# A DeltaNet and FFN kernel on one core: scores of the first two chunks in two parts, the first inverse's fill ahead of its load, and a new order list

## The chip, the core and the metric

The kernel runs on one core of one Trainium2 chip. Five engines run their own instruction streams and wait for each other by semaphores: TensorE (PE; its weight loads are counted apart as PEld), VectorE (DVE), ScalarE (ACT), GpSimd (POOL) and SyncE (SP), which issues every DMA of this kernel. The metric is the time of one execution on the device in microseconds; less is better. The kernel before took 546.81 us, the median of three runs (544.82 to 550.54).

## The reference

```python
def _attn_ref(q, k, v, beta):            # (4, 8, 768, 48), beta (4, 8, 768), float32
    k_n = k / (np.linalg.norm(k, axis=-1, keepdims=True) + 1e-06)
    state = np.zeros((B, H, D, D))
    for t in range(S):
        kt, vt, bt = k_n[:, :, t], v[:, :, t], beta[:, :, t, None]
        y[:, :, t] = np.einsum('bhd,bhde->bhe', q[:, :, t], state)
        v_old = np.einsum('bhde,bhd->bhe', state, kt)
        state = state + bt[:, :, :, None] * np.einsum('bhd,bhe->bhde', kt, vt - v_old)
    return y

x = attn_out.transpose(0, 2, 1, 3).reshape(3072, 384)
a = x @ w1                               # w1, w2: 384 x 1024, float64
b = x @ w2
h = a * b @ w3                           # w3: 1024 x 1024
out = h @ w_out                          # w_out: 1024 x 384
```

A recurrence over 768 tokens gives, for 4 batches and 8 heads, a state of 48 x 48 and an output for each token. Its result, 3072 x 384, goes through a feed-forward block with a product of two projections in the middle. The weights come as 64-bit floats.

## The kernel before

**Attention.** The 768 tokens are cut into 12 chunks of 64, and pairs of chunks make 6 units. In a chunk the recurrence becomes matrix products: scores of keys with keys (times beta and the norms they give a triangular matrix U) and of queries with keys (masked, the tile PT), the inverse of the triangular matrix, and a chain over the chunks that carries the state. For a chunk m the parts are called `k`, `q`, `v` (loads), `K` and `Q` (transposes of keys and queries into the tile KQ on TensorE, `by_tensor`, chunks 0 and 1), `p` and `d` (the same for later chunks, by a permuted load of eight DMAs and VectorE's transpose), `s` (`scores`: TensorE, then VectorE writes U, then PT), `u` (`to_blocks`: U into the layout of the inverse), `e` (`corner`: TensorE builds the whole inverse from its blocks), `n`, `c` (the chain) and `y` (outputs). For a unit j there are `g` and `N` (squares and norms; `N` ends with the weights wt, on which U depends) and `V` (`inverse`).

**The inverse** of a unit is done in 32 x 32 blocks, all of them side by side: a load of U into the tile Ub, a fill of a pair of PSUM banks with the unit matrix by ScalarE (two copies, L516 and L521), 31 steps of two VectorE operations each, and a way back. In units 0 and 1 the load is a VectorE transpose (L508) of columns that ScalarE (four copies for a unit) and GpSimd (two) wrote before it (L492); in units 2 to 5 it goes through DRAM: eight DMAs write Ud (L499) and one loads Ub (L510). The bank pair stays taken until the inverse is done.

**Weights.** 36 pieces `P0` to `P35` (P0 to P7 of w_out, P8 to P23 of w3, then w1 and w2) are converted from 64-bit words on the chip: a DMA into one of five raw buffers, a pair of ScalarE operations (L837, L840), a VectorE shift (L842) and a GpSimd add (L844). `t` transposes a piece of w3 on TensorE (L880) and copies it to w3T, `f` multiplies w3 with w_out (`fold`, eight products of 384 columns in two halves, L895). The first fold takes the w_out pieces in the order 0, 3, 2, 5, then 1, 4, 6, 7.

**The feed-forward block** of unit 0 is done directly (`a`, `b`, L915). Units 1 to 5 use a scheme with fewer products over sums of tokens and weights (`m`, L1117, with additions on VectorE at L1143 and L1148, on ScalarE at L1145 and on VectorE or GpSimd at L200), and `o` (L1199) multiplies with the folded weights.

**Order.** Each part is a Python generator. The string ORDER names parts, and each name advances that part to its next `yield`; so the list sets the order of instructions on each engine. A stroke behind a name (`t2'`) gives that step to the other engine (ScalarE or VectorE for copies, GpSimd or VectorE for sums), and `+3` puts three matmuls whose result nobody reads ahead of the step. `bank` hands out four PSUM banks in turn, `two_banks` pairs of others. Each DMA takes one of eight semaphores in turn, so at most eight are under way.

```python
turn = (0, 3, 2, 5, 1, 4, 6, 7) if first else (0, 3, 2, 1, 5, 4, 6, 7)
for i, kc in enumerate(turn):
    pe.matmul(
        ps[:, 0:DM], lhsT=w3Ts[jc, kc // 4][:, kc % 4 * P : kc % 4 * P + P],
        rhs=wo[:, kc], start=(i == 0), stop=(i == KF - 1),
    )
    if i == KF // 2 - 1:
        yield
```

Of the kernel before, what the change touches and what calls it, by code (L numbers as in the profile page):

```python
# [12 lines left out]
ALU = mybir.AluOpType  # L13
# [26 lines left out]
warm+3 P11 beta P2 P0 P11 P11 P11 P2 beta P3 k0 K0 P0 beta P0 P0 K0' K0 P6 P6 k1 K1 zd zd zd P2 g0 P2 P9 P3  # L40
q0 K0 K0 g0 g0 g0 g0 g0 P6 P9 g0 g0 K1 P9 P3 K1 P16 K1 q1 Q0 P10 Q0' N0 K1' P6 P16 P16 P3 Q0 Q0 Q0
P12 P13 P10 s0 N0 s0 P9 P5 s0 Q1 P10 P12 Q1' P16 zp zp P12 Q1' Q1 s0 Q1' P13 P8 p2 P5 P10 t3 s0 P13
P13 s0 s0 P1 P12 u0 u0 s1 s1 s1 s1 s1 s1 P7 P4 t2 t2' t3' u0 t5 t4 P5 t5' u1 u1 u1 V0 P8 P5 V0 P8 f1
P8 V0 t1 t1 t4 t0 t8 P17 d2 zp zp zp zp zp V0 V0 V0 V0 P14 k2 P1 P1 P1 t0 N0 t8 P4 P15 V0 P7 V0 V0
V0 P7 P17 V0 P4 V0 V0 V0 P17 P7 P4 P17 f2 f0 f2 f1 V0 s1 P14 d2 V0 V0 V0 k3 P14 P15 f2 V0 s0 g1 f0
f1 g1 P14 g1 t6 t9 P19 P18 P19 f0 t9 v0 V0 V0 g1 V0 P15 V0 P19 g1 P15 P19 zp t6 P18 P23 P22 v1 f4 f4
t7 t11 t7 V0 V0 V0 t11 g1 g1 P22 P23 f3 V0 P18 V0 V0 V0 V0 g1 P26 n0 P18 t10 V0 P23 V0 P22 V0 P20
t10 N1 n0 f3 P26 f5 f5 f3 e0 N1 e0 e0 e0 e0 p2 P20 P23 P22 d2 d2 P20 e1 e0 s2 f4 p3 P21 p3 P24 P25
e0 e0 P20 n1 t12 t15 P26 f5' s2 s2 d3 c0 c0 e1 t14 s2 e1 t14 t12 t15' P21 y0 s2 s2 d3 c0 f7 y0 P26
d3 P21 P21 d3 e1 u2 u2 u2 s1 n1 e1 c0 e1 s3 s3 s3 s3 s3 s3 y0 P27 t13 P29 c1 c1 t13' e1 P24 f6 u3 u3  # L50
u3 V1 V1 V1 V1 V1 P24 V1 V1 V1 P28 P24 e1 c1 c1 P25 P27 V1 P27 V1 P29 f7 p4 P32 y1 f7 f6 y1 P25 V1
V1 V1 V1 V1 V1 y1 P28 P25 P28 P27 b0 b0 v2 P30 P31 P28 f6 d4 V1 P29 P29 zp V1 V1 V1 P32 b3 b1 b2 b1
b3 b2 b7 d4 V1 V1 P32 V1 V1 V1 V1 b7 b4 a07 c1 a04 a07 a04 b4 a02 a00 a01 P30 a05 a02 V1 V1 V1 V1 V1
V1 V1 V1 V1 a00 n2 n2 P32 a01 P31 P30 P31 a05 a03 b5 e2 e2 e2 N1 a03 P31 P33 a06 c1 k4 p4 e2 P35 P34
k5 c2 P30 e2 d4 c2 P33 b5 d4 a00 b3 e3 g2 b3 p5 e2 a06 e2 P33 a00 g2 g2 g2 P33 b2 a03 e3 e2 P34 e3
c2 a03 c2 P35 P34 g2 P35 a02 a02 g2 b2 y2 b0 d5 e3 b0 d5 a01 g2 s4 P34 W y2 v3 P35 p5 g2 a01 N2 N2
b6 a06 b6 T T W T b6 b4 W a06 e3 n3 W s4 s4 s4 s4 d5 s4 d5 a04 e3 s4 b7 b6 b4 b7 s5 s5 s5 s5 s5 T s5
u4 v4 b5 a05 W W n3 n4 e3 s5 b5 a04 W' W S0 u5 V2 e3 c2 N2 V2 c2 V2 a07 c3 b1 a05 c3 b1 V2 V2 c3 c3
V2 a07 V2 V2 V2 V2 V2 oA0 V2 V2 y3 S0 S0' W W S0 S0 S0 n4 S0 xA0 oA0 oD0 W p6 S0 S0 S0 S0 y3 S0 S0
S0 y3 S0 xA0 oB0 oC0 V2 V2 V2 V2 V2 G1 V2 xB0 oB0 S0 G1 G1 G1 G1 c3 xA0 m10 d6 V2 V2 V2 V2 V2 xB0  # L60
xC0 oC0 xD0 m10 m10 G1 G1 G1' m10 m10 m10 m10 k6 d6 xC0 V2 V2 W xC0 V2 p6 V2 xD0 xC0 V2 W V2 m10 W
m10 m10 m10 W V2 V2 m10 m10 m10 V2 m10 m10 V2 W' m10 V2 V2 k7 W W G1 m10 m10 G1 c3 V2 e4 W m10 m10
m10 m10 m10 m10 g3 m10 m10 g3 m10 m10 m10 m10 m10 d6 g3 m10 W g3 g3 e4 g3 c4 G1 m10 m10 m10 m10 e4
c4 m10 d6 p7 m10 m10 m10 m11 e4 e4 g3 g3 G1 m10 e5 m10 m11 m11 s4 e4 c4 c4 m10 m10 m10 m10' N3 m11
# [39 lines left out]
def kernel(  # L104
# [313 lines left out]

    Ux = padded("U", [P, 2 * NR * H * C + 8], 1, 2 * NR * H * C)[0]
    Us = [Ux[:, NR * H * C * i : NR * H * C * (i + 1) + 8] for i in range(2)]  # L420

    def scores(m):
        u = Us[m % 2][:, 0 : NR * H * C].rearrange("p (r h t) -> p r h t", r=NR, h=H)
        for r in range(NR):
# [978 lines left out]
```

## Time and profile before

| | before |
|---|---|
| median of three runs | 546.81 us (544.82 to 550.54) |
| the profiled execution, and its span | 541.17 us, 539.5 us |
| mean granted clock of TensorE | 0.978 |
| TensorE busy | 513.8 us (95%) |
| VectorE, ScalarE, GpSimd busy | 403.2, 221.5, 274.7 us |
| DMA | 52.66 MB in 197593 packets, mean 98 GB/s |

The span runs from the first to the last instruction of the profiled execution. Rows of a timeline give the start, the duration, the engine, the line of the kernel, the operation with its output and inputs, their shapes, a count of instructions, and in brackets the idle time of the engine ahead of the row with what ended it. "issue" means that nothing the profile shows was waited for. A matmul in float32 leaves two records.

### The profile page before, as it was taken

What the parts mean: (1) busy time and instruction counts of PE and PEld (TensorE: products, weight loads), DVE (VectorE), ACT (ScalarE), POOL (GpSimd) and SP (SyncE); (2) the same over time, 40 slices, a digit from 0 to 9 for tenths busy, and PEclk for the clock granted to TensorE, in tenths of its full rate; (3) what the DMA queues carried; (4) which work ended last, traced back from release to release, by engine and by line L of the source; (5) the groups of instructions that cost most, each with busy time, mean ns of one, the idle gap of its engine ahead of it and who ended that gap; (6) DMA issues with size and microseconds to landing.
All of it is one profiled execution on the core that took longest, in us unless ns stands there. A gap on an engine that the chain in (4) does not pass through costs nothing.

```text
span 539.5 us, 19915 instructions
## 1 busy us (share of the span) xinstructions
PE 513.8 (95%) x8466; PEld 431.6 (80%) x8466; DVE 403.2 (75%) x880; ACT 221.5 (41%) x453; POOL 274.7 (51%) x296
## 2 busy tenths in 40 slices
PE   6679998999999999999999999999999999999997
PEld 3555567688888988889988889878899788997886
DVE  2689986898667997869987799887879845536562
ACT  3787586747523133532134333245321342312210
POOL 4575763344889996066932258361368302051150
PEclk7599998999999999999999999999999999999999
DMA  8979974767554264654444561644314320010001
GB/s 222 239 202 237 239 112 114 154 163 151 98 84 81 60 139 65 104 108 78 103 102 61 82 114 49 137 80 56 53 52 108 76 40 4 17 51 8 2 1 60
DMA packets 197593, 52.66 MB, mean 98 GB/s; under 512 B 184576, under 2 KB 191872, under 8 KB 197504
## 3 DMA queue, kind: packets, MB, share of 16 engines
q1 hardware_dynamic: 197504, 51.38, 46.1%
q8 instruction: 67, 1.10, 0.9%
q14 instruction: 22, 0.18, 0.1%
HBM read 41.25 MB, written 8.91 MB: 93 GB/s over the span
## 4 chain that ended last, share of the span: by engine, by line
PE 65%; DVE 14%; SPq 7%; DMA 6%; ACT 3%; issue 3%; POOL 1%; DVEq 0%; ACTq 0%; POOLq 0%
PE ps_f L1117 26%; PE ps_f L1199 20%; PE ps_w L687 5%; SPq L297 4%; PE ps_f L895 3%; PE ps_w L786 3%; DVE tb L530 3%; DVE ps_w L535 3%; PE ps_f L915 2%; DVE KQ L390 2%; PE ps_w L616 2%; DMA raw<-in_moe_w_dram 2%; DMA perm<-in_q_dram 1%; PE ps_w L433 1%; SPq L269 1%
## 5 line engine op out<-in xcount | busy, mean ns | idle before, releaser
L200 POOL TENSOR_TENSOR ab<-ab 128x512 f32<-128x512 f32 (+1 forms) x57 | 65.5, 1167 | 67.5 <-DVE ab L1148 33.7
L1199 PE MATMUL ps_f<-w,ab 128*128 128x192 f32 x376 | 65.1, 327 | 0.0
L1117 PE MATMUL ps_f<-xT,w1s 128*128 128x256 f32 x240 | 63.4, 388 | 0.1
L1117 PE MATMUL ps_f<-xT,w2s 128*128 128x256 f32 x240 | 61.7, 387 | 1.4 <-DVE x_room L1148 1.0
L1199 PEld LDWEIGHTS ps_f<-w,ab 128*128 128x128 f32 x376 | 61.9, 190 | 0.7
L1148 DVE TENSOR_TENSOR ab<-ab,ps_f 128x512 f32<-128x512 f32 x70 | 47.6, 682 | 17.1 <-PE ps_f L1117 15.4
L1117 PEld LDWEIGHTS ps_f<-xT,w1s 128*128 128x128 f32 x240 | 43.5, 189 | 9.6 <-ACT x_room L1145 1.8
L1117 PEld LDWEIGHTS ps_f<-xT,w2s 128*128 128x128 f32 x240 | 43.6, 189 | 9.3 <-DVE x_room L1148 1.7
L459 POOL TENSOR_TENSOR PT<-PT,smask 128x512 f32<-128x512 f32 x20 | 25.4, 1276 | 44.9 <-ACT PT L457 44.7
L1199 PE MATMUL ps_f<-room,ab 128*128 128x192 f32 x272 | 47.2, 329 | 0.0
L546 DVE TENSOR_TENSOR ps_w<-ps_w,tb 128x31 f32<-128x31 f32 (+15 forms) x124 | 43.3, 349 | 4.5
L895 PE MATMUL ps_f<-w2s,w3T 128*128 128x384 f32 x128 | 43.8, 492 | 1.5 <-POOL w2s L844 1.0
L1199 PEld LDWEIGHTS ps_f<-room,ab 128*128 128x128 f32 x272 | 44.2, 190 | 0.5
L541 DVE TENSOR_TENSOR tb<-ps_w,Ub 128x31 f32<-128x31 f32 (+15 forms) x124 | 41.8, 337 | 3.4 <-DMA Ub<-Ud 0.3
L805 ACT COPY xT<-ps_w 48x256 f32<-48x256 f32 x96 | 30.6, 366 | 33.4 <-PE ps_w L786 32.9
L200 POOL TENSOR_TENSOR xT<-xT 128x256 f32<-128x256 f32 x44 | 31.9, 740 | 20.6 <-DVE xT L200 14.7
L1117 PE MATMUL ps_f<-xT,room 128*128 128x256 f32 x160 | 39.9, 381 | 0.0
L895 PEld LDWEIGHTS ps_f<-w2s,w3T 128*128 128x128 f32 x128 | 23.4, 190 | 17.3 <-POOL w2s L844 2.4
L1148 DVE TENSOR_TENSOR x_room<-x_room,ps_f 128x512 f32<-128x512 f32 x40 | 27.2, 679 | 11.1 <-PE ps_f L1117 10.0
L1145 ACT COPY x_room<-ps_f 128x512 f32<-128x512 f32 x20 | 11.7, 586 | 55.6 <-PE ps_f L1117 45.3
L1117 PEld LDWEIGHTS ps_f<-xT,room 128*128 128x128 f32 x160 | 30.1, 190 | 4.1
L1145 ACT COPY ab<-ps_f 128x512 f32<-128x512 f32 x20 | 11.7, 586 | 49.7 <-PE ps_f L1117 49.6
(196 smaller groups left out, 1078.5 us busy)
## 6 DMA issues: line engine op xcount, KB each, us to landing
raw<-in_moe_w_dram SPq DMA_DIRECT2D x16, 512.0 KB, 5.8
ktok<-in_k_dram SPq DMA_DIRECT2D x48, 96.0 KB, 3.4
vtok<-in_v_dram SPq DMA_DIRECT2D x24, 192.0 KB, 4.2
raw<-in_moe_w_dram SPq DMA_DIRECT2D x24, 192.0 KB, 4.3
out_dram<-osb SPq DMA_DIRECT2D x46, 96.0 KB, 1.7
raw<-in_moe_w_out_dram SPq DMA_DIRECT2D x8, 384.0 KB, 4.2
perm<-in_k_dram SPq DMA_DIRECT2D x40, 64.0 KB, 3.0
perm<-in_q_dram SPq DMA_DIRECT2D x32, 64.0 KB, 2.6
```

The costliest lines, as they stand in the source:

```text
L200: (dve if other else pool).tensor_tensor(out=out, in0=x, in1=y, op=op)
L297: sync.dma_start(out=dst[quarter(2 * e + j), :, :, tb, 0:nd].rearrange("t b a d -> t (b a) d"), in_=src.rearrange("b (a e) t d -> e (b a) ...
L459: pool.tensor_tensor(out=PT, in0=PT, in1=smask[:].unsqueeze(1).to_broadcast([P, H, C]), op=ALU.mult)
L541: dve.tensor_tensor(out=tv, in0=V[:, 0 : s + 1, s : s + 1].to_broadcast([P, s + 1, n]), in1=U[:, s, s + 1 : BS].unsqueeze(1).to_broadcast( ...
L546: dve.tensor_tensor(out=o, in0=o, in1=tv, op=ALU.subtract)
L687: pe.matmul(out(ps, r, h, z), lhsT=lhs(r, h, z), rhs=rhs(r, h, z), start=True, stop=True,)
L805: act.copy(out=xT[f, cc, p:NP:2, b : b + NR, :].rearrange("p a r t -> p r a t"), in_=pyv[f, z, b : b + NR],)
L895: pe.matmul(ps[:, 0:DM], lhsT=w3Ts[jc, kc // 4][:, kc % 4 * P : kc % 4 * P + P], rhs=wo[:, kc], start=(i == 0), stop=(i == KF - 1),)
L1117: pe.matmul(ps[:, n * g : n * g + n].rearrange("p (b c t) -> p b c t", b=HB, c=2), lhsT=product_weights(i, 2 * r + g), rhs=of[i], start=na ...
L1145: act.copy(out=t, in_=cell(what[1]))
L1148: dve.tensor_tensor(out=t, in0=t, in1=cell(what[2]), op=op)
L1199: pe.matmul(ps[b][:, b, :], lhsT=block(u, HF * f + i, z)[:, P * b : P * b + P], rhs=ws_[w][:, i], start=first and i == 0 and (b == 0 or n ...
```

## The change

It has three parts. First, the scores of chunks 0 and 1 are made by a new function, `early_scores`. The key products of both token groups of a chunk go into one bank pair, with two VectorE operations behind them that write U (part `s0`, `s1`, five yields fewer than before). The query products, ScalarE's copy to PT and GpSimd's mask are parts of their own, `h0` and `h1`. In the even heads a 128-column product (keys and queries beside each other) becomes two of 64 columns. Second, the inverse of unit 0 fills its banks ahead of its load. Third, ORDER is written anew from its first to its last line.

```diff
 ORDER = """
-warm+3 P11 beta P2 P0 P11 P11 P11 P2 beta P3 k0 K0 P0 beta P0 P0 K0' K0 P6 P6 k1 K1 zd zd zd P2 g0 P2 P9 P3
-q0 K0 K0 g0 g0 g0 g0 g0 P6 P9 g0 g0 K1 P9 P3 K1 P16 K1 q1 Q0 P10 Q0' N0 K1' P6 P16 P16 P3 Q0 Q0 Q0
...
+zd zd zp zp P10 P10 P10 P10 beta beta beta P0 P0 P0 P0 k0
+K0 k1 K0 P16 zd P16 g0 g0 g0 g0 P16 P16 K1 K1' K1 K0'
...
+    def by_weight(m, r, x):
+        u = Us[m % 2][:, 0 : NR * H * C].rearrange("p (r h t) -> p r h t", r=NR, h=H)
+        dve.tensor_tensor(
+            out=by_parity(u[:, r]), in0=x,
+            in1=by_parity(scale_of(ws, m)[:, r].unsqueeze(2)).to_broadcast([P, NP, 2, C]),
+            op=ALU.mult,
+        )
+
+    def early_scores(m, j):
+        KQ = KQs[m]
+        ps = two_banks()
+        fill(ps[:, 0])
+        for r in range(NR):
+            for h in range(H):
+                for z in range(2):
+                    x = KQ[feat(h % 2), NR * z + r, h // 2]
+                    n = 128 * (h // 2) + C * r
+                    pe.matmul(
+                        ps[half(z ^ (j if h % 2 else 0)), h % 2, n : n + C],
+                        lhsT=x[:, 0, :], rhs=x[:, j, :], start=True, stop=True,
+                    )
+        yield
+        psv = ps[:].rearrange("p e (a r t) -> p a e r t", a=NP, r=NR)
+        if j == 0:
+            for r in range(NR):
+                by_weight(m, r, psv[:, :, :, r, :])
+                yield
+            return
+        PTs[m] = in_turn(work, [P, NR, H, C], "PT", 3, "PT")
+        for r in range(NR):
+            act.copy(out=by_parity(PTs[m][:, r]), in_=psv[:, :, :, r, :])
+            yield
+            by_mask(PTs[m][:, r])
+            yield
...
     def inverse(j):
+        def load():
+            if j in TURNED:
+                dve.transpose(out=U[:], in_=columns().rearrange("p t m g -> p t (m g)"))
+            else:
+                sync.dma_start(out=U[:], in_=Uds.pop(j)[:])
+
         U = in_turn(work, [P, BS, BS], "Ub", 1, "Ub")
-        if j in TURNED:
-            dve.transpose(out=U[:], in_=columns().rearrange("p t m g -> p t (m g)"))
-        else:
-            sync.dma_start(out=U[:], in_=Uds.pop(j)[:])
-        yield
+        if j:
+            load()
+            yield
...
+        if j == 0:
+            load()
+            yield
...
-        parts[f"s{m}"] = lambda m=m: scores(m)
+        parts[f"s{m}"] = lambda m=m: scores(m) if m > 1 else early_scores(m, 0)
...
+        parts[f"h{m}"] = lambda m=m: early_scores(m, 1)
```

Lines of the new kernel lie 47 to 85 behind those of the old: L445 (U) becomes L476, L492 becomes L570, L508 becomes L586, L516 and L521 become L598 and L603, L530 and L535 become L615 and L620, L837 to L844 become L922 to L929, L880 becomes L965, L895 becomes L980. The rows that follow give an instruction's line, operation, output and inputs, the size, and a count.

On VectorE, from the first U to the first inverse step, stood before (U_103 is the tile U, w and w2s are weight pieces):

```order
L445 TENSOR_TENSOR U_103<-ps_w,wt 128x512
L842 TENSOR_SCALAR w_330<-w_330 128x512
L204 COPY KQ<-ps_f 48x8x64
L842 TENSOR_SCALAR w_420<-w_420 128x512
L204 COPY KQ<-ps_f 48x8x64 x2
L842 TENSOR_SCALAR w_432<-w_432 128x512
L445 TENSOR_TENSOR U_103<-ps_w,wt 128x512 x3
L204 COPY w3T<-ps_f 128x512 x2
L842 TENSOR_SCALAR w2s<-w2s 128x384
L204 COPY w3T<-ps_f 128x512
L508 STREAM_TRANSPOSE Ub<-xT_79 128x1024
```

and stands now, from the norm weights on:

```order
L417 TENSOR_TENSOR wt<-wt,ps_f 128x32
L927 TENSOR_SCALAR w_322<-w_322 128x512
L927 TENSOR_SCALAR w2s<-w2s 128x384
L476 TENSOR_TENSOR U_103<-ps_w,wt 128x512
L251 COPY KQ<-ps_f 48x8x64
L476 TENSOR_TENSOR U_103<-ps_w,wt 128x512 x3
L927 TENSOR_SCALAR w_407<-w_407 128x512
L927 TENSOR_SCALAR w2s<-w2s 128x384
L927 TENSOR_SCALAR w_403<-w_403 128x512
L251 COPY KQ<-ps_f 48x8x64
L927 TENSOR_SCALAR w2s<-w2s 128x384
L251 COPY KQ<-ps_f 48x8x64
```

One KQ copy and no weight shift is left between the first U and the other three, where three of each stood. Behind the last U come shifts and copies, then the transpose (L586).

On ScalarE, around the columns of unit 0 and the fill of the first inverse, stood before (PT is the query scores, eye the unit matrix):

```order
L457 COPY PT<-ps_w 128x512
L492 COPY xT_79<-U_103 96x32x16
L457 COPY PT<-ps_w 128x512
L492 COPY xT_79<-U_103 32x32x16
L492 COPY xT_79<-U_103 96x32x16
L492 COPY xT_79<-U_103 32x32x16
L837 ACTIVATE w_574<-raw 128x512
L840 ACTIVATE raw<-raw 128x512
L516 COPY ps_w<-eye 128x1023
L521 COPY ps_w<-eye 128x1
L204 COPY w3T<-ps_f 128x512 x2
```

and stands now:

```order
L570 COPY xT_79<-U_103 32x32x16
L922 ACTIVATE w_562<-raw 128x512
L925 ACTIVATE raw<-raw 128x512
L251 COPY w3T<-ps_f 128x512
L504 COPY PT<-ps_w 128x512 x2
L598 COPY ps_w<-eye 128x1023
L603 COPY ps_w<-eye 128x1
L363 COPY wt<-wt 128x16
L365 COPY wt<-wt 64x16 x2
L922 ACTIVATE w2s<-raw 128x384
L925 ACTIVATE raw<-raw 128x384
L251 COPY w3T<-ps_f 128x512 x2
```

The PT copies come behind the last column copy, and the fill behind them; the pair on `w2s` behind the three norm copies is piece P5 of w_out.

On SP, around the permuted loads of chunk 2, stood before (P5 is the single w_out row, ahead of them):

```order
L829 DMA raw<-in_moe_w_out_dram 128x768
L829 DMA raw<-in_moe_w_dram 128x1024
L297 DMA perm_95<-in_k_dram 32x16x32 x2
L297 DMA perm_95<-in_k_dram 32x16x16 x2
L297 DMA perm_95<-in_k_dram 32x16x32 x2
L297 DMA perm_95<-in_k_dram 32x16x16 x2
L829 DMA raw<-in_moe_w_out_dram 128x768 x3
```

and stands now:

```order
L914 DMA raw<-in_moe_w_out_dram 128x768
L914 DMA raw<-in_moe_w_dram 128x1024
L344 DMA perm_95<-in_k_dram 32x16x32 x2
L344 DMA perm_95<-in_k_dram 32x16x16 x2
L344 DMA perm_95<-in_k_dram 32x16x32 x2
L344 DMA perm_95<-in_k_dram 32x16x16 x2
L914 DMA raw<-in_moe_w_out_dram 128x768
L914 DMA raw<-in_moe_w_dram 128x1024
L914 DMA raw<-in_moe_w_out_dram 128x768 x3
```

The w_out row directly behind the permuted loads is P5 now, and a w3 piece, P8, and three more w_out pieces, with P1 the first of them, follow it. The w_out row ahead of the loads is another piece.

180 lines of the change are left out of this document (111 added, 69 removed).

## The prediction

> **What bounds the kernel now.** I read the page's busy times first, then the stretches, then the engines' rows where TensorE is idle.
>
> ```profile
> span 539.5 us, 19915 instructions
> PE 513.8 (95%) x8466; PEld 431.6 (80%) x8466; DVE 403.2 (75%) x880; ACT 221.5 (41%) x453; POOL 274.7 (51%) x296
> ```
>
> TensorE works for 513.8 of 539.5 us. A new order can win only the other 25.7 us, and time lost to a low clock. The table by stretches (start:end, length, then busy time of PE, PEld, DVE, ACT and POOL, the granted clock, the DMA share and GB/s) tells where these are:
>
> ```profile
> 0.00:13.50 13.50, 8.14 (x84) 4.79 (x84) 3.64 (x8) 5.05 (x8) 6.36 (x17) 0.80 0.88 222
> 13.50:27.00 13.50, 8.14 (x202) 6.88 (x206) 8.81 (x26) 9.60 (x20) 6.95 (x9) 0.50 0.98 240
> 27.00:40.50 13.50, 10.46 (x216) 7.92 (x209) 11.29 (x20) 11.37 (x17) 9.74 (x8) 0.94 0.73 200
> 67.50:81.00 13.50, 12.70 (x270) 8.58 (x268) 10.82 (x33) 10.75 (x18) 8.94 (x9) 1.00 0.72 111
> 81.00:94.40 13.40, 12.03 (x381) 9.88 (x382) 8.34 (x14) 9.37 (x18) 5.21 (x6) 0.87 0.48 114
> 94.40:108.00 13.60, 12.56 (x327) 8.61 (x319) 11.67 (x31) 10.50 (x20) 4.91 (x4) 1.00 0.76 153
> 108.00:515.00 407.00, 404.03 (x6798) 350.27 (x6797) 312.30 (x667) 145.19 (x315) 208.91 (x218) 1.00 0.40 77
> ```
>
> The first three rows hold 5.4 + 5.4 + 3.0 = 13.8 us of idle TensorE, 67.5 to 108 holds 0.8 + 1.4 + 1.0 = 3.2, the 407 us of the body only 3.0; the rest lies mostly at the very end. The change aims at the start. There two lines of work run toward the first corner product e0 at 74.97, and TensorE's rows (start, duration, count, and in brackets the idle time and its releaser; a matmul leaves two records) show one of them:
>
> ```profile
> 39.99 0.91 PE L895 MATMUL ps_f<-w2s,w3T 128*128 128x384 f32 x2 [0.75 <-POOL w2s L844]
> 41.90 1.26 PE L880 MATMUL ps_f<-ident,w 128*128 128x128 f32 x8 [0.56 <-POOL w L844]
> 43.00 5.97 PE L895 MATMUL ps_f<-w2s,w3T 128*128 128x384 f32 x18
> 74.97 0.73 PE L616 MATMUL ps_w<-T,U 33*33 33x32 f32 x62
> ```
>
> These are the folds w3·w_out. From 43.00 on TensorE has 44 of their products (0.66 us each: 5.97 us over 9) and five transposes (0.6: 1.26 over two) before e0: 29.0 + 3.0 of the 32.0 us. So e0 comes at 75 if the second half of the first fold starts at 43 and nothing else holds it. The other line is VectorE's: scores times weights (L445, the tile U), U turned into columns (L492), the transpose (L508), 31 inverse steps (L530, L535), the transpose back (L549), then T for e0.
>
> ```profile
> 27.47 0.19 DVE L370 TENSOR_TENSOR wt<-wt,ps_f 128x32 f32<-128x32 f32 x1
> 28.37 0.42 DVE L842 TENSOR_SCALAR w<-w 128x512 uint32<-128x512 uint32 x1
> 35.10 0.69 DVE L445 TENSOR_TENSOR U<-ps_w,wt 128x512 f32<-128x512 f32 x1 [1.26 <-PE ps_w L439]
> 38.87 1.25 DVE L508 STREAM_TRANSPOSE Ub<-xT 128x1024 f32<-128x1024 f32 x1 [0.36 <-POOL xT L492]
> 41.11 0.19 DVE L530 TENSOR_TENSOR tb<-ps_w,Ub 128x31 f32<-128x31 f32 x1
> 73.97 0.70 DVE L599 STREAM_TRANSPOSE T<-TT 128x512 f32<-128x512 f32 x1
> ```
>
> T is done at 74.67, 0.3 us before TensorE reaches e0. **Both lines end together**: to bring e0 forward the change must shorten both.
>
> **The inverse's line.** Its start hangs on loads. 13.73 MB in the first 60 us are 229 GB/s:
>
> ```profile
> DMA packets 22506, 13.73 MB, mean 229 GB/s; under 512 B 19707, under 2 KB 19707, under 8 KB 22499
> raw<-in_moe_w_dram SPq DMA_DIRECT2D x14, 512.0 KB, 5.9
> raw<-in_moe_w_out_dram SPq DMA_DIRECT2D x8, 384.0 KB, 4.2
> ktok<-in_k_dram SPq DMA_DIRECT2D x16, 96.0 KB, 5.0
> 14.76 1.94 PE L404 MATMUL ps_f<-ident,ktok 64*48 64x64 f32 x58 [0.58 <-DMA ktok<-in_k_dram]
> 20.21 1.95 PE L404 MATMUL ps_f<-ident,X 64*48 64x64 f32 x62 [1.46 <-DMA X<-in_q_dram]
> ```
>
> Adding the bytes queued up to the end of k1 (one w3 piece, beta, four w_out pieces, eight k loads: 2.9 MB, 12.7 us) and 2.5 us for the start and the last landing gives 15.2 where the row shows 14.8, so the estimate is good to a microsecond. Afterwards one w3 and one w_out piece stand ahead instead (1.8 MB): k1 at 10.4, q0 at 14.4 instead of 20.2. The norm weights, 27.66 before, follow k1 by a few operations and come at about 21.5. Now all four U are due at once, since their key products no longer stand behind Q1 and the second chunk's halves: four of 0.69 us and four other VectorE operations in between give 25.5 for the last, 10 us earlier than 35.79.
>
> Little of that arrives. ScalarE and GpSimd do the column copies behind other rows:
>
> ```profile
> 33.73 1.12 ACT L492 COPY xT<-U 96x512 f32<-96x512 f32 x1
> 34.74 0.60 ACT L457 COPY PT<-ps_w 128x512 f32<-128x512 f32 x1
> 35.37 3.34 ACT L492 COPY xT<-U 32x512 f32<-32x512 f32 x3
> 38.73 0.67 ACT L837 ACTIVATE w<-raw 128x512 f32<-128x512 f32 x1
> 39.31 0.66 ACT L840 ACTIVATE raw<-raw 128x512 uint32<-128x512 uint32 x1
> 39.87 1.01 ACT L516 COPY ps_w<-eye 128x1023 f32<-128x1023 f32 x1
> 37.75 1.08 POOL L492 COPY xT<-U 32x512 f32<-32x512 f32 x1
> 38.92 1.02 POOL L844 TENSOR_TENSOR w2s<-w2s,raw 128x384 uint32<-128x384 uint32 x1
> ```
>
> ScalarE's four copies (4 x 1.11) stand among piece conversions (a pair is 1.3, for the narrower w_out pieces 1.0) and two KQ copies (0.6 like the PT copy) and end at some 32.5. GpSimd's two stand behind five adds (1.0 for 384 columns, so some 1.35 for 512) and six memsets, and the second ends at about 34.2. The transpose then ends at 35.4. The fill, 1.0 and a short second copy (0.2, as the 32-column row of VectorE), comes behind the columns, a conversion pair (1.3), a w3T copy and two PT copies (0.6 each), and ends at 36.8. It is ahead of the transpose only in the list. So the first inverse step comes at 36.8, not 41.11: **4.3 us earlier**. The bounds are 0 (the copies stay behind GpSimd's adds) and 12 (two copies and the transpose follow U at once: 25.5 + 2.2 + 1.3).
>
> **The folds' line.** Here P5, the w_out piece of the first fold's fourth product, moves on SP from ahead of the eight perm DMAs to behind them:
>
> ```profile
> 22.32 0.38 SPq L829 DMA_DIRECT2D raw<-in_moe_w_out_dram  x1
> 25.89 7.54 SPq L297 DMA_DIRECT2D perm<-in_k_dram  x8
> ```
>
> These take 7.54 us from about 25, so P5 is issued at about 32.5 and lands at 36.7 (4.2 above). Its ScalarE pair (1.0) now stands behind the fill and three small norm copies (0.2 each) and ends at 38.5. VectorE's shift and GpSimd's add (0.4 and 1.0) give 39.9, and that fourth product was at 39.99 before. P1, for the second half, follows with its pair behind two w3T copies and P8's pair (38.5 + 1.1 + 1.3 + 1.0 = 41.9), then 0.4 and 1.0: 43.3, against 43.00. Then the same 44 products and five transposes come: e0 at **75.3, +0.3**. The bounds are -2 (P1 meets no queue) and +3 (P5 and P1 each meet one 1.3 us operation more). T, 4.3 us earlier at about 70.4, then waits for TensorE.
>
> **Score matmuls.** 32 products of 128 columns become 64 of 64. They lie before the folds, where TensorE idles 13.8 us, and cost 0 there; uncovered, 32 more at the 0.06 us apart of the 64-column row at 20.21 (1.95 over 31) would be 2 us, kept as bound. Warm-up matmuls (three, 4.29 us at the half clock at 1.65) go from the start to the gap before the first fold, where TensorE would wait for P13.
>
> ```profile
> 1.65 4.29 PE L194 MATMUL ps_f<-ident 128*128 128x512 f32 x6 [1.65 <-POOL ident masks.py:199]
> ```
>
> The clock was 0.50 from 13.5 to 27 us, though, and 0.94 in the next stretch, where matmuls stood thicker. If the score products end by 27 and only transposes follow, the folds may start at 0.5. [...]
>
> **After e0.** The largest waits of 67.5 to 108 are these:
>
> ```profile
> 81.80 0.31 PE L687 MATMUL ps_w<-vtok,TT 64*64 64x48 f32 x2 [1.51 <-issue]
> 95.25 0.73 PE L687 MATMUL ps_w<-S,KQ 48*64 48x48 f32 x35 [0.67 <-issue]
> ```
>
> They are "issue" waits inside or between products with no releaser: an earlier chain does not free them, a new order may. The clock of 0.87 costs 0.13 x 13.4 = 1.7 more. Bounds -4 (all of these) and +2 (one more such drop); I take -0.6, the size of the shorter one.
>
> **The body and the end.** The body's list is new throughout, with 3.0 us of idle to win. Units 2 to 5 load their inverse through DRAM, and VectorE's first step waits there:
>
> ```profile
> 385.21 0.68 DVE L445 TENSOR_TENSOR U<-ps_w,wt 128x512 f32<-128x512 f32 x1
> 394.63 0.19 DVE L541 TENSOR_TENSOR tb<-ps_w,Ub 128x31 f32<-128x31 f32 x1 [0.15 <-DMA Ub<-Ud]
> ```
>
> The way from U to the first step is 8.7 us in unit 5. The new list puts the first steps directly behind load and fill. Summed from the durations of such rows, VectorE has about 6.5 us of work between in unit 2, 9.5 in unit 3, 10 in unit 4 and 7 in unit 5, so it stands waiting about 2 us each in units 2 and 5, with the evacuations of TensorE's banks queued behind. Four rotating banks cover most: +0.5, bounds -2 (most of the idle time) and +4 (both waits reach TensorE). The last two units' products keep their order on TensorE: 0 (bounds -0.5 and +0.5).
>
> Sum: +0.3 + 0 - 0.6 + 0.5 + 0 = +0.2 on the profiled execution's 541.17 gives 541.4. The median of the three runs was 546.81, 5.6 above; with the same distance the time is **547.0**. A change of 1% (5.5 us) is about what a measurement of this kernel can tell.
>
> **Rivals.** *Faster: both lines move.* If P1 is ready by 41 and the clock is full by the first fold, e0 comes 2 earlier; with the waits and the low clock of 81 to 94 gone (-3.2) and 1.5 won in the body, the time is 547 - 6.7 = 540. For it: 13.8 us of idle lie there to be used. Against: P5 stands behind the perm loads.
> *Slower: the weight conversions arrive late.* One mechanism at one place: P5 and P1 are at the end of the queues of SP, ScalarE and GpSimd. Each microsecond after 43.3 goes one to one into e0, as TensorE has no slack from there to 75. If the perm DMAs start 3 us later because the raw buffer ahead of them is not free, and the clock costs the folds what it costs the stretch from 81 (1.7), e0 comes at 80, and with 2 of waits in the body: +7, 554. It decides from P1's add ending at 48.
> *It does not do what it says*: U comes early, but the column copies keep their place behind conversions and the inverse starts at 41. Folds and inverse end together as before: 547 to 549.
>
> **How the numbers follow.** The first case (hidden behind the folds) has 0.42, with its own range 543.5 to 550.5. No earlier inverse has 0.10, the faster rival 0.23, the slower 0.25. Within 1% are the first and the third, with some of the rivals' near ends: 0.54; faster 0.22, slower 0.24. The range of 539.5 to 553.5 reaches to the faster rival's time and to just short of the slower's, with about a tenth left out on each side.
>
> **What would show it.** Last U near 25.5 (hidden or not), first inverse step near 37, fourth fold product near 40, second half of the first fold near 43.3, e0 near 75.3, T ready some 4 us before. If e0 stands at 72 or 79, the fold's line is mis-sized. If e0 is right and the time is off by over 3 us, the body's list is: then the idle time of TensorE between 108 and 515, now 3.0, shows it by releaser.

## The result and the profile after

The changed kernel takes 553.61 us (median of 16 runs, 550.54 to 560.5), the kernel before 546.46 in the same series. The ratio is **1.0147, with a 95% interval of 1.0122 to 1.0173**: slower by some 8 us. (This ratio and those below leave out executions that lie over 1.5% above the fastest of the same kernel, so they are not quite the quotient of the medians.) The forecast was 547.0 with a range up to 553.5.

The profiled execution took 554.23 us, its span 552.5. From the page of the changed kernel (busy time of PE, PEld, DVE, ACT, POOL; the instruction queue q8: packets, MB, share):

```profile
span 552.5 us, 20019 instructions
PE 515.7 (93%) x8530; PEld 432.7 (78%) x8530; DVE 406.6 (74%) x883; ACT 221.9 (40%) x454; POOL 269.4 (49%) x292
q8 instruction: 67, 1.10, 0.9%
```

The start went nearly as worked out up to the first inverse step and the folds. VectorE's and TensorE's rows of the changed kernel:

```profile
24.75 1.89 DVE L476 TENSOR_TENSOR U<-ps_w,wt 128x512 f32<-128x512 f32 x3
35.45 1.23 DVE L586 STREAM_TRANSPOSE Ub<-xT 128x1024 f32<-128x1024 f32 x1
37.01 0.19 DVE L615 TENSOR_TENSOR tb<-ps_w,Ub 128x31 f32<-128x31 f32 x1 [0.33 <-ACT ps_w L603]
39.89 0.63 PE L965 MATMUL ps_f<-ident,w 128*128 128x128 f32 x4 [1.26 <-ACT w3T L251]
40.35 2.78 PE L980 MATMUL ps_f<-w2s,w3T 128*128 128x384 f32 x8
43.41 13.07 PE L980 MATMUL ps_f<-w2s,w3T 128*128 128x384 f32 x40
75.41 0.76 PE L701 MATMUL ps_w<-T,U 33*33 33x32 f32 x64
```

The last U ends at 26.6, the first inverse step is at 37.01, 4.1 us earlier than before, the next run of fold products at 43.41, and e0 at 75.41 where it was at 74.97. So 0.4 us of the loss lies ahead of e0, and all the rest behind it. The stretches of the changed kernel behind e0 (length, then busy time of PE, PEld, DVE, ACT, POOL, clock, DMA share, GB/s):

```profile
76.00:108.00 32.00, 26.33 (x765) 19.49 (x752) 20.84 (x41) 23.93 (x40) 18.21 (x17) 0.89 0.67 139
108.00:515.00 407.00, 399.01 (x6872) 343.50 (x6871) 310.75 (x670) 144.75 (x316) 198.91 (x211) 1.00 0.42 78
```

and the first of them in the kernel before:

```profile
76.00:108.00 32.00, 28.79 (x877) 22.13 (x878) 22.89 (x49) 23.61 (x44) 14.60 (x14) 0.95 0.66 139
```

TensorE stands idle 2.5 us longer from 76 to 108, and 5.0 us longer in the body (3.0 before, 8.0 now). Its long waits there have one thing in common, the word in the brackets:

```profile
83.13 0.27 PE L965 MATMUL ps_f<-ident,w 128*128 128x128 f32 x1 [3.22 <-issue]
96.96 0.21 PE L525 MATMUL ps_w<-KQ 48*64 48x64 f32 x1 [1.06 <-issue]
159.40 0.33 PE L525 MATMUL ps_w<-KQ 48*64 48x64 f32 x3 [1.46 <-issue]
242.16 0.27 PE L525 MATMUL ps_w<-KQ 48*64 48x64 f32 x2 [1.64 <-issue]
373.42 0.44 PE L772 MATMUL ps_w<-S,KQ 48*64 48x48 f32 x13 [0.79 <-issue]
```

The profile shows no semaphore that held these matmuls. All issue waits of over 0.15 us behind e0 sum to 8.6 us, against 2.5 in the kernel before; waits for another engine sum to 4.0 against 2.8. The clock's own rows have 10.2 us at half speed behind e0 (from 85, 98 and 160 on), against 3.4, which by estimate is another (10.2 - 3.4) / 2 = 3.4 us: in the kernel before, pairs of 128-column score records start 0.21 us apart at 25.18 to 26.03, at half speed, and 0.11 apart at 29.12 to 29.34, at full. Together with e0: 6.1 + 1.2 + 3.4 + 0.4 = 11.1 of the 13.0 us between the two spans; the other 1.9 us I can't assign. The two profiled executions stand further apart than the medians.

**The theory, F.** The instruction queue moved 67 packets of 16 KB. TensorE's 8530 matmul records and as many weight loads make 17060 instructions, 255 a packet; that these are what the packets hold is read from this count, and the expectations take it as 256. A float32 matmul leaves two matmul records and two weight loads, four instructions, so a block, as such a packet is called here, holds some 64 matmuls. By the packets' times in the trace, each long issue wait ends 2.2 to 3 us after such a packet starts: at 80.60, 94.05, 157.15, 239.85 and 370.96 for the five rows above. So by this theory TensorE waited for its own instructions. The changed kernel has 32 more score matmuls, half a block, and a new list, so the blocks begin at other instructions. **The rival, O**: the waits belong to the order of the work, and would come wherever blocks begin.

### The profile page after: what moved, and what is told of

The parts are those of the page before. It is cut to its first block, busy times and chain, and to the rows that moved or that the text cites. A ratio compares the mean times of both kernels' runs of the same rounds, so it can differ in the third digit from the quotient of the medians.

```text
span 552.5 us, 20019 instructions
## 1 busy us (share of the span) xinstructions
PE 515.7 (93%) x8530; PEld 432.7 (78%) x8530; DVE 406.6 (74%) x883; ACT 221.9 (40%) x454; POOL 269.4 (49%) x292
## 4 chain that ended last, share of the span: by engine, by line
PE 67%; DVE 12%; SPq 7%; DMA 6%; issue 5%; POOL 2%; ACT 1%; DVEq 0%; POOLq 0%; ACTq 0%
PE ps_f L1202 29%; PE ps_f L1284 15%; PE ps_w L772 6%; PE ps_f L1000 5%; SPq L344 4%; PE ps_w L871 3%; PE ps_w L701 2%; PE ps_f L980 2%; PE ps_w L519 2%; DMA raw<-in_moe_w_dram 2%; DVE tb L626 1%; DVE ps_w L620 1%; DVE tb L615 1%; PE ps_w L525 1%; DVE ps_w L631 1%
## 5 line engine op out<-in xcount | busy, mean ns | idle before, releaser
L1202 PEld LDWEIGHTS ps_f<-xT,w1s 128*128 128x128 f32 x240 | 43.1, 189 | 11.1 <-ACT x_room L1230 1.8
L631 DVE TENSOR_TENSOR ps_w<-ps_w,tb 128x31 f32<-128x31 f32 (+15 forms) x124 | 43.3, 349 | 4.5
L980 PE MATMUL ps_f<-w2s,w3T 128*128 128x384 f32 x128 | 44.7, 502 | 0.3 <-issue 0.3
L980 PEld LDWEIGHTS ps_f<-w2s,w3T 128*128 128x128 f32 x128 | 24.2, 196 | 16.1 <-issue 2.1
L437 DVE STREAM_TRANSPOSE KQ<-perm 128x512 f32<-128x512 f32 x36 | 24.4, 696 | 12.0 <-PE ps_w L871 4.7
```

The costliest lines, as they stand in the source:

```text
L437: dve.transpose(out=KQ[:, bs, :, i, :].rearrange("p b a t -> p (b a) t"), in_=src[:, bs].rearrange("p b a x d -> p (b a) (x d)"),)
L631: dve.tensor_tensor(out=o, in0=o, in1=tv, op=ALU.subtract)
L980: pe.matmul(ps[:, 0:DM], lhsT=w3Ts[jc, kc // 4][:, kc % 4 * P : kc % 4 * P + P], rhs=wo[:, kc], start=(i == 0), stop=(i == KF - 1),)
L1202: pe.matmul(ps[:, n * g : n * g + n].rearrange("p (b c t) -> p b c t", b=HB, c=2), lhsT=product_weights(i, 2 * r + g), rhs=of[i], start=na ...
```

## The experiments

### Half a block at the start of the kernel before

```diff
-warm+3 P11 beta P2
+warm+3 pad P11 beta P2
...
+    def pad():
+        ps = bank([P, CW])[:]
+        for _ in range(32):
+            pe.matmul(ps[0:BS, 0:BS], lhsT=ident[0:BS, 0:BS], rhs=ident[0:BS, 0:BS],
+                      start=True, stop=True)
+        for _ in range(3):
+            skip("f")
+        yield
```

> The kernel before with 32 small unread matmuls (32x32) at its idle start, behind the warm-up: 128 instructions of TensorE more (four to a float32 matmul), half of one 16 KB instruction block, and nothing else. Theory F (the issue waits are late instruction blocks: 67 packets of 16 KB in the instruction queue are 17152 instructions, and the long issue waits of both traces end 2.2 to 3 us after such a packet starts): the blocks now begin elsewhere in the same order, so the issue waits after 75 us, 2.5 us in the profile before (1.51, 0.32, 0.67), come at other places and with another sum, anything from 0 to 8 us, and the time moves by as much. Theory O (the waits belong to the order of the list): the same issue waits at the same places, 2.5 us, time 546.5 within 1 us (the 32 matmuls take some 2 us of TensorE's idle time).

Measured: 550.85 us, ratio **1.0154 (1.0093 to 1.0216)**. The matmuls themselves took 2.2 us, in idle time, and e0 came at 75.16, 0.2 later than before. Behind it, in the same order of work, stand these waits:

```profile
81.04 0.33 PE L927 MATMUL ps_f<-ident,w 128*128 128x128 f32 x1 [2.13 <-issue]
98.66 0.26 PE L663 MATMUL ps_w<-TT,late 64*33 64x32 f32 x1 [2.10 <-issue]
373.36 0.68 PE L734 MATMUL ps_w<-vtok,TT 64*64 64x48 f32 x31 [1.53 <-issue]
```

The issue waits sum to 6.8 us, at other instructions than before, and 6.8 us ran at half clock. Theory F's forecast came, theory O's did not: filler that is as good as free at its own place costs as much as the whole change. Whether any filler at the start costs, wherever the blocks lie, is asked further down.

### The two halves of the two lists

The list of the one kernel up to e0's first product, and the other's remaining steps in their order behind it: above, the changed list goes on with the old one, below it the old list with the changed one. The second of the three has 32 unread matmuls ahead of Q0 in addition, so that with the 32 more of the scores it is one block off, not half a block.

```diff
 e0 e0 e0 e0 P20 e0
-P22 P22 P22 p3 d2 P20 d2 e0
+P22 P22 P26 P23 P22 n0 P26 f3
...
 e0 N1 e0 e0 e0 e0
-p2 P20 P23 P22 d2 d2 P20 e1
+zp f4 P20 p2 f5 n1 P20 p3
```

> The changed kernel up to the first corner product e0 of its list, and from there the list of the kernel before (with the query scores of chunk 1 at their old place). The start of the changed list cost 0.4 us up to e0, so theory O (the loss lies in the new list behind e0) gives 546 to 547.5 and idle times as before: 3.2 us between 67.5 and 108, 3 us in the body. Theory F: the 32 more score matmuls put the instruction blocks half a block off against the kernel before, so the issue waits behind e0 are not those of before; the time may lie anywhere from 544 to 553. Had the start after all been what costs (a colder clock, a fuller DMA queue behind e0), it would be 553.

> The same with 32 small unread matmuls at TensorE's idle time ahead of the first query transposes: 64 matmuls more than before in all, one whole instruction block, so behind e0 the blocks begin at the same instructions as in the kernel before. Theory F: the issue waits behind e0 are those of before again (about 1.5 at the first state products and 0.7, 2.5 us in all), time 546 to 548. Theory O: the same as without the 32.

> The kernel before up to e0 and from there the changed list. Theory O: the loss is all in the part behind e0, so 552 to 554, with the waits of the changed kernel (3.2 us idle near 80, 1.5 near 158, 1.6 near 241). Theory F: the blocks begin half a block off against the changed kernel, so the issue waits differ in place and size; between 544 and 553, and what is left of the loss with issue waits set aside (0.5 to 0.6 us waits for GpSimd and VectorE) is under 2.5 us.

Measured: 1.0198 (1.0132 to 1.0264) for the new start with the old rest, 1.014 (1.007 to 1.021) with the filler, 1.0191 (1.0137 to 1.0246) for the old start with the new rest. Theory O is out in its plain form: the new start with the old rest should have been as fast as before, and lost 2%. But 554.0 us for the new start is close to the 553 expected if the start costs by what it leaves behind e0, and 552.3 us for the new rest is what theory O expected. Theory F missed its own mark with the new rest: the span, 548.6, lies 9.1 us above the one before; the issue waits make 4.1 - 2.5 = 1.6 of it and waits for other engines 7.4 - 2.8 = 4.6, so far more than 2.5 us is left with the issue waits set aside.

Theory F is not cleanly shown by the run with the filler either. The filler stood in the wrong place: it took 3.59 us at 17.77, and the key products behind it stopped for 3.34 us more, until 2.9 us after an instruction packet had started at 25.54:

```profile
28.41 1.55 PE L491 MATMUL ps_w<-KQ 48*64 48x64 f32 x47 [3.34 <-issue]
```

So the last three U began at 30.02, not 25.68, though the norm weights were there no later (23.14 and 23.56), and e0 came at 79.96 where it was at 75.79 without. From e0 to the end it takes 471.1 us (551.1 - 79.96) against 477.6 without, 477.1 in the changed kernel and 464.5 before. It has issue waits of 0.9 us only, less than the 2.5 expected, but 8.3 us of waits for other engines and 10.2 us at half clock. Without the 5.1 us that the half clock costs, 466.0 us are left, as with the old start at such a place (466.7 and 468.3 us in two runs further down, with next to no half clock). So nothing there says that the new start costs behind e0 by itself, but for a colder clock, which this run can't exclude.

### A whole block at the start, with nothing else changed

The three wide warm-up matmuls (12 instructions) give way to 67 small ones (268), which take 7.35 us at 1.65 where the three took 4.29; the list is otherwise that of the kernel before.

```diff
-warm+3 P11 beta P2
+pad P11 beta P2
...
-        for _ in range(32):
+        for _ in range(67):
```

> The kernel before with its three warm-up matmuls replaced by 67 small unread ones (32x32): 12 instructions go, 268 come, 256 more in all, exactly one instruction block, in about the same 5 us of TensorE's idle start. Behind them every block begins at the same instruction as in the kernel before. Theory F: the issue waits are those of the kernel before again (about 1.5 at the first state products near 80 and 0.7 near 95, 2.5 us behind 60 us), one or two stretches of half clock behind 60 us, and the time is 544 to 548 where half a block gave +7.5. Theory P (any filler at the start costs, by the clock, the loads or the order of arrival, not by the blocks): again +5 to +8, 551 to 554.

Measured: 544.7 us beside 545.0, ratio **1.000 (0.9956 to 1.0043)**. Half a block costs 1.5%, a whole one nothing. The start was put off by as much in both: the first matmuls on beta began at 9.11 with half a block and at 9.06 with a whole one, 6.01 before, so it isn't filler as such that costs. The largest issue wait stands at the same instruction as before, ahead of the last two records of the state products; this is the row of the kernel with the whole block, beside the one at 81.80 in the prediction:

```profile
81.67 0.31 PE L734 MATMUL ps_w<-vtok,TT 64*64 64x48 f32 x2 [0.84 <-issue]
```

Its sum of issue waits was smaller than expected, 0.8 us, and it had more waits for other engines (7.6 us) in the profiled execution, so that the spans differ by 4 us while the times of the runs do not.

### Quarters of a block, in both kernels

In the kernel before the warm-up gives way to 19 or 51 small matmuls (64 or 192 instructions more); in the changed kernel 16, 32 or 48 stand ahead of everything, while TensorE waits for beta.

```diff
-warm+3 P11 beta P2
+pad P11 beta P2
```

```diff
-zd zd zp zp P10
+pad zd zd zp zp P10
```

> The kernel before with its three warm-up matmuls replaced by 19 small unread ones: 64 instructions more behind them, a quarter of a block; the list is unchanged. Theory F (instruction blocks): waits of its own, anything from 544 to 558; with the other three places (546 for none, 550.9 for a half, and the next run) it tells whether the old list is better than the new one at all places or only at its own. Theory that only the old list's own place is good: 549 to 555.

> The same with 51, three quarters of a block. The new list had ratios of 1.0147, 1.032, 1.017 and 1.015 at its four places (mean 1.020). If the old list's mean over its four places is 1.005 or less, the new list loses about 1.5% by itself (its dense products stand closer together, whatever the place); if it is 1.012 or more, at least half of the loss is the old list's lucky place.

> The changed kernel with 16 small unread matmuls ahead of everything, while TensorE waits for beta: 64 instructions, a quarter of a block. Theory F: the issue waits (8.5 us behind 60 us in the changed kernel: 3.22, 0.32, 1.06, 1.46, 1.64, 0.79) change in place and sum, each still ending 2.2 to 3 us after an instruction packet starts; the time moves by as much, 547 to 558. Theory O (the new list itself costs): 553.6 within 1.5 us, the same waits.

> The same with 32 (half a block). Theory F: other waits again, between 546 and 558; theory O: 553.6 within 1.5 us.

> The same with 48 (three quarters of a block). Theory F: other waits again, between 546 and 558; theory O: 553.6 within 1.5 us. If over the four places of the blocks the changed kernel's mean stays above 550, its list is worse than the old one on the whole; if one of the four comes to 547 or less, the place of the blocks alone makes the loss.

| blocks moved by | old list, ratio | new list, ratio |
|---|---|---|
| 0 | 1 | 1.0147 (1.0122 to 1.0173) |
| a quarter | 1.0073 (1.0026 to 1.0119) | 1.0317 (1.0245 to 1.039) |
| a half | 1.0154 (1.0093 to 1.0216) | 1.0172 (1.011 to 1.0233) |
| three quarters | 1.0112 (1.0061 to 1.0163) | 1.015 (1.0116 to 1.0184) |
| a whole | 1.000 (0.9956 to 1.0043) | not run |
| mean of the first four | 1.0085 | 1.0197 |

The old list was at its best place, and no other of these four reaches it. The new list loses at each of its four, and no place brings it to 547 or less. Neither of the two marks set for the old list's mean, 1.005 and 1.012, is reached: it lies between. The loss of 1.47% can be put as 1.12 (difference of the means) + 0.85 (the old list's own place against its mean) - 0.50 (the new list's own place against its mean). Part of the 1.0317 is not the blocks' doing, since e0 came at 77.86 there, 2.4 us late; without it the new list's mean would be some 0.1% less. Theory F's range for a quarter block in the new list, 547 to 558 us, was missed: it took 563.27. Issue waits alone don't make the new list worse in the mean: behind e0 they are 8.6, 11.8, 5.7 and 5.2 us at its four places, but 2.5, 6.8 and 7.5 at none, a half and three quarters of the old one (one execution each). No run took the new list apart at a fixed place; a pair of traces below shows one more part of the difference.

### The two parts of code without the new list

The changed code with the old list: the first three steps of s0 and s1 stand where these stood, and h0 and h1 where their other five did. The warm-up gives way to 35 small matmuls, and with the 32 more of the scores that is a whole block.

```diff
-warm+3 P11 beta P2
+pad P11 beta P2
...
 Q1' Q1
-s0
+h0
 Q1' P13
...
-P13 s0 s0 P1 P12 u0 u0 s1 s1 s1 s1 s1 s1
+P13 h0 h0 P1 P12 u0 u0 s1 s1 s1 h1 h1 h1
```

> The two changes of code alone, scores in two parts and the fill ahead of the load, with the old list (the first three steps of s0 and s1 stand where those stood, the other five as h0 and h1 where the rest stood), and the warm-up replaced by 35 small matmuls, so that with the 32 more score matmuls one whole block is added. By theory F the blocks behind e0 begin where they did: 545 to 548, e0 at 75 to 76 (the folds bind, the code parts are hidden). If the two parts of code cost by themselves: 549 or more with e0 at 77 or later.

Measured: 545.56 beside 545.11, ratio **1.000 (0.9967 to 1.0033)**. The scores in two parts and the early fill neither win nor lose by themselves. Here are its e0 and its largest issue wait, at the same state products as in the kernel before:

```profile
77.10 0.73 PE L701 MATMUL ps_w<-T,U 33*33 33x32 f32 x62
84.55 0.31 PE L772 MATMUL ps_w<-vtok,TT 64*64 64x48 f32 x3 [2.13 <-issue]
```

e0 came at 77.1, 2.1 us later than before and later than expected, and the time was the same all the same.

### The changed kernel once more

> The changed kernel once more, for a second profile. Theory F: the same issue waits at the same instructions (L965 near 80, L525 near 96, 158 and 241, L772 near 373), each within some tenths of 3.2, 1.1, 1.5, 1.6 and 0.8 us. If they are chance, they lie elsewhere.

Measured: 552.43 us, 1.0117 (1.0058 to 1.0175). The second profiled execution has a span of 546.5 us instead of 552.5. Its waits stand at the same instructions, down to the count of records behind them:

```profile
79.82 0.27 PE L965 MATMUL ps_f<-ident,w 128*128 128x128 f32 x1 [0.96 <-issue]
93.32 0.21 PE L525 MATMUL ps_w<-KQ 48*64 48x64 f32 x1 [0.79 <-issue]
155.17 0.33 PE L525 MATMUL ps_w<-KQ 48*64 48x64 f32 x3 [0.92 <-issue]
235.25 0.27 PE L525 MATMUL ps_w<-KQ 48*64 48x64 f32 x2 [0.26 <-issue]
366.53 0.44 PE L772 MATMUL ps_w<-S,KQ 48*64 48x48 f32 x13 [0.49 <-issue]
```

So in these two executions their places are fixed by the program. Their sizes are not (3.22 became 0.96, 1.64 became 0.26, and there is one more of 1.19 at 84), against what was expected. Nothing behind e0 ran at half clock this time. Waits of 5.3 instead of 8.6 us and 5.1 us less of lost clock (10.2 / 2) are more than the difference of the two spans: this is how far executions of one kernel lie apart.

This trace can be held against the one of the section before: the same code in the old list (but for the warm-up), as many matmul records behind e0, both at full clock. From e0 to the end, first the old list, then the new:

```profile
77.10:543.80 466.70, 452.38 (x7857) 390.68 (x7856) 345.59 (x734) 170.63 (x361) 230.28 (x237) 1.00 0.40 79
74.36:546.50 472.14, 455.36 (x7856) 390.53 (x7856) 350.58 (x739) 173.12 (x364) 226.26 (x233) 1.00 0.40 78
```

The new list takes 5.4 us longer. 3.0 us of it is not waiting but busy time of TensorE, for the same products in another order, and 2.4 us is idle time, with issue waits of 5.3 against 2.3 us. (The ends of matmuls are modelled in a profile, so 3.0 is an estimate.) What in the order makes it is not shown.

### What makes a block late

First, 64 small matmuls, a whole block, at two places of the old list: ahead of the first product of s8, and ahead of a product of m30 that begins a bank.

```diff
-c6 c6 s8 m21 m21
+c6 c6 s8+64 m21 m21
...
-m30
+m30+64
```

> The kernel before with 64 small unread matmuls (one whole block each) at two places of the body: ahead of the first scores of chunk 8, near 290 us, between the chain's and the scores' small products, and ahead of a wide feed-forward product of unit 3, near 330 us, between products of 256 columns. By their rows at the start each takes 2.2 us by itself. Theory D (the blocks come too late only where many small products follow each other, since a block of 256 instructions is used up faster than the next one comes): an issue wait of over 0.8 us with or right behind the 64 at 290, none over 0.3 at 330. Theory Q (a block is late because data transfers are ahead of it, whatever is computed): waits by what SP moves there, not by the place.

Measured: 557.35 us, 1.0213 (1.0116 to 1.031), and the time a block of these takes was expected wrongly. The 64 took 4.2 to 4.8 us, not 2.2 (the row of the start was for 32). The second of the places came at 359.4, not near 330. There was a wait of 0.24 us at the first place and none at the second:

```profile
292.04 2.24 PE L242 MATMUL ps_w<-ident 32*32 32x32 f32 x65
294.51 2.34 PE L242 MATMUL ps_w<-ident 32*32 32x32 f32 x63 [0.24 <-issue]
```

Theory D (blocks are late only among many small products) is not supported by it, but it wasn't tested either: the shortest time between two instruction packets in all traces is 3.3 us, and a block that takes 4.2 us to use up can come in time.

Then 192, three blocks, at two places among wide products, in m30 and in m51, and faster: they alternate between partitions 0 to 31 and 64 to 95, and took 17 ns a record (152 in 2.59 us, in the rows below) where those of the run before took 34 (65 in 2.24 us):

```diff
-m30
+m30+192
...
-m51
+m51+192
...
+                x = slice(C * (i % 2), C * (i % 2) + BS)
+                pe.matmul(
+                    ps[x, 0:BS], lhsT=ident[x, x], rhs=ident[x, x],
+                    start=True, stop=True, skip_group_check=True,
+                )
```

> The kernel before with 192 unread 32x32 matmuls (three whole blocks) at each of two places among the wide products of 256 columns: in unit 3, near 357 us, and in the last unit, near 500 us, where hardly any data is moved (DMA share 0.02). They alternate between the two halves of the array, as the corner's products do, which took 0.73 us for 64 records. In the run before this the 64 at one place were no fair test: they ran one behind the other, 4.2 us to a block, and the shortest time between two instruction packets in all traces is 3.3 us. Theory R (TensorE waits wherever it uses up blocks faster than one in 3.3 to 4 us, data transfers or not): at some 11 to 17 ns a record the three blocks are used up in 4 to 7 us, and issue waits of 2 to 6 us in sum come at both places. Theory Q (a block is late only when data transfers are ahead of it): no wait over 0.3 near 500.

Measured: 568.28 us, 1.0435 (1.0241 to 1.0628). In the timeline of TensorE, at the two places:

```profile
348.22 2.59 PE L243 MATMUL ps_f<-ident 32*32 32x32 f32 x152
352.15 2.48 PE L243 MATMUL ps_f<-ident 32*32 32x32 f32 x128 [1.33 <-issue]
356.15 2.98 PE L243 MATMUL ps_f<-ident 32*32 32x32 f32 x104 [1.52 <-issue]
...
521.24 4.67 PE L243 MATMUL ps_f<-ident 32*32 32x32 f32 x270
527.71 3.11 PE L243 MATMUL ps_f<-ident 32*32 32x32 f32 x114 [1.81 <-issue]
```

and the two stretches, of which the first moves next to no data (DMA share 0.02, behind the clock):

```profile
520.00:531.00 11.00, 9.19 (x391) 8.35 (x390) 1.37 (x2) 0.12 (x1) 1.26 (x1) 0.86 0.02 4
349.00:360.00 11.00, 8.14 (x350) 7.75 (x343) 0.14 (x1) 0.00 (x0) 1.27 (x1) 0.72 0.40 93
```

The waits came at both places, 2.9 us in sum at the one and 1.8 at the other, the last a little under what was expected. **Theory R's forecast came: TensorE waited where it used up its instructions faster than blocks come (128 records with their weight loads, a block, in 2.48 us at 352.15, where packets start 3.3 us apart at the least), with data transfers beside it or without.** That transfers lengthen such a wait is not excluded, as the place with a DMA share of 0.40 has the longer ones.

Nor is fast use the only way to such a wait. The longest one of the changed kernel, 3.22 us at 83.13, came after a stretch of wide fold products:

```profile
53.70:80.60 26.90, 24.68 (x260) 15.71 (x259) 24.18 (x67) 15.31 (x29) 17.56 (x19) 1.00 0.84 172
```

One packet had started at 53.68, the next started only at 80.60, 0.7 us after TensorE had stopped, with twice the instructions of a block used in between (260 matmul records and 259 weight loads). The packet was late there though nothing was used up fast. The DMA engines' share was 1.03 from 75 to 80.6; that data transfers held the packet up (theory Q) fits, and is not tested. In 22 of the 82 waits counted below, the packet before lies over 8 us back.

## Why the prediction was wrong

**Right: the time of e0.** Last U 26.6 (25.5 forecast), first inverse step 37.01 (36.8), fold products from 43.41 (43.3), e0 75.41 (75.3). The rival "it does not do what it says" fell in its cause, an inverse that starts at 41, though its outcome, that folds and inverse end together, came (see below). The first fold was late: its fourth product began at 42.3 where 40 was said, as the fold itself began only at 40.35, behind a wait of 1.26 us for a w3T copy; what follows did not move with it.

**Luck: the working behind 43.3.** The prediction takes the products there for the second half of the first fold, which needs P1. But the list goes `f1`, `t0`, `f2`: at 43.41 stands the first half of the second fold, with pieces 0, 3, 2, 1 in turn, and P1 is first used at 45.34. Its add ended at 44.60, 1.3 us later than said, and cost nothing. The row at 43.41 follows directly on the transposes of `t0` at 42.97. The prediction's row of the kernel before, at 43.00, is the second fold too.

**Wrong: "T, 4.3 us earlier", hidden behind the folds.** These are VectorE's transposes back (the kernel before, then the changed one) and the changed kernel's T, which was at 73.97:

```profile
69.36 1.24 DVE L549 STREAM_TRANSPOSE Ub<-ps_w 128x1024 f32<-128x1024 f32 x1
69.45 1.24 DVE L634 STREAM_TRANSPOSE Ub<-ps_w 128x1024 f32<-128x1024 f32 x1
74.65 0.70 DVE L684 STREAM_TRANSPOSE T<-TT 128x512 f32<-128x512 f32 x1
```

The inverse began 4.1 us earlier and ended when it had ended before. From its first step to the transpose back VectorE took 32.4 us instead of 28.3: the new list gives it more work in between (29.7 us busy, 26.7 before), and it waits 0.9 us for a piece of ScalarE at 38.87. T was done at 75.35, not 70.4, and 0.06 us ahead of e0. Both lines end together again, so the 4 us were not hidden but spent; e0 came right because the folds' line did.

**Wrong, and the step that failed: what lies behind e0.** The sum has "after e0" at -0.6 and the body at +0.5, together -0.1 us. From e0 to the end the changed kernel took 477.1 us, and 472.1 in the second execution, against 464.5. The row of 1.51 <-issue was seen and read as something that "a new order may" free; no bound let such waits grow, since the +2 there stands for the clock. It was the first sign of a price: issue waits behind e0 grew from 2.5 to 8.6 us (5.3 in the second execution), and the clock cost 3.4 us more (nothing in the second). From 76 to 108 the idle time grew by 2.5 us, and the clock fell from 0.95 to 0.89, 1.9 us more by 0.06 x 32. The time without a releaser should have been a mechanism of its own in the sum, with a price on both sides, not a remainder. The prediction's last sign, e0 right and the time off by over 3 us, pointed to this place.

**Wrong: the term for the score matmuls, as a rule.** The step said that they "cost 0 there", since TensorE idles where they stand, and bounded them by the time they take. Their own time is free indeed (1.000 with a whole block). But by theory F the 128 instructions move the begin of every block behind them, and 32 matmuls with no use and no wait cost 1.5% in the old list. What this shift cost in the new list is not shown: with half a block more, which makes the shift a whole one, it took 1.0172, no less than 1.0147. The measured loss is 1.1% between the means of the two lists, 0.85% for the old list's good place, and 0.5% back; the first of the three stays open but for the 3.0 us of busy time.

**Wrong in size: the body, +0.5 with a bound of +4.** TensorE's idle time from 108 to 515 grew by 5.0 us, 3.9 of it in the three issue waits at 159, 242 and 373, and 3.4 us at half clock from 160 on cost 1.7. VectorE's waits for Ub were there as said, but smaller: 1.8 us in all, the longest 1.2, where two of about 2 were expected.

**The slower case had a chance of 0.24, for a reason that did not happen: P1's add ended at 44.60, not at 48.** Half of its second reason, the clock, was right: half clock did cost, in 3.4 us pieces, but behind e0 and not at the folds: there the clock was full from 30.1 on, ahead of the three warm-up matmuls at 35.17. The row of 4.29 us in the prediction is no pure half clock either: its first three records took 1.06 to 1.22 us and its last two 0.59, and the clock's first row, at full, begins at 4.6.

## What to carry to other kernels

In these traces every "issue" wait of TensorE of over 0.3 us behind 60 us reads as a wait for its own instructions (82 waits, each ending 2.2 to 3.2 us after a packet starts); compare the end of such a wait with the instruction queue's packets before an order is blamed. In this kernel, with many small float32 matmuls one behind the other, 128 instructions added at the start moved the issue waits behind e0 to other instructions (2.5 us of them became 6.8) and cost 1.5%. So an edit of the order of such a kernel is to be measured at several places of the blocks (filler of a quarter, a half and three quarters at an idle place), or its own effect can't be told from this one, which is up to 1.5% in the old list here. Whether breaking such runs with wide products wins was not tried.

## What the runs showed of the hardware that was not expected

**Instructions come in blocks, and they can be late.** In all 16 traces there are 82 issue waits of over 0.3 us behind 60 us, and each of them ends 2.2 to 3.2 us after a packet of the instruction queue q8 starts; two such packets never start closer than 3.3 us to each other. In the median they start 5.4 us apart there, so that a band of 1 us is no chance. What fixes the start of a packet is not shown. In the changed kernel q8 moved 67 packets of 16 KB, and behind e0 the six waits of over 0.3 us took 8.5 us of the profiled execution.

**A stretch of small matmuls did not keep the clock up.** In the run with 64 of 32x32 at each of two places, TensorE was busy 7.76 of 8 us around the first of them, and then ran at half clock for 6.8 us:

```profile
289.00:297.00 8.00, 7.76 (x218) 7.04 (x210) 4.77 (x18) 3.00 (x8) 2.65 (x3) 0.95 0.37 57
297.00:303.00 6.00, 6.00 (x80) 4.69 (x80) 1.31 (x2) 1.67 (x3) 2.49 (x2) 0.50 0.01 3
```

So the clock fell here behind no more than 0.24 us of idle time. At the second place, 64 in a row from 359.38 for 4.23 us, it stayed full. In this trace all changes of the clock lie whole multiples of 3.413 us apart. Of the stretches of 3.413 us counted off from these changes, the one from 292.85 to 296.26 held small matmuls alone, but for a wait of 0.24 us, while the two around 361.12 held wide products too. That this is the difference is argued from two places, not shown. The pieces at half clock behind e0 are 3.4, 6.8 or 10.2 us long in every trace, but for a last one at the end of the kernel: one, two or three times 3.413 us.
